# Attention of the first batch in two sweeps over the head pairs, with two loads a pair

## The chip, the cores and the metric

The kernel runs on one core of a Trainium2 chip. Its time is the device time of one execution, in microseconds (us). The engines are TensorE (PE in the rows, its weight loads PEld), VectorE (DVE), ScalarE (ACT), GpSimd (POOL) and SyncE (SP), on whose queue all loads and stores are issued.

## The reference

Three layers follow each other, for B=4 batches of S=576 tokens with H=8 heads of D=64:

```python
a = softmax(causal(q @ k.T / sqrt(D)))
mem = (phi(q) @ M_prev) / (phi(q) @ z_prev + 1e-6)       # phi(x) = elu(x) + 1
x = (sigmoid(beta) * mem + (1 - sigmoid(beta)) * (a @ v)) as [2304, 512]
P = exp(x @ w_gate - max); 8 rounds of row and column normalization
x = sum over e of P[:, e] * (relu(x @ w1[e]) @ w2[e])    # 8 experts, inner width 1024
out = leaky(x @ w_in) @ w_out                            # inner width 2048
```

## The kernel before

**Attention.** `Attention.run` goes over 16 units, a unit being one batch `b` and one pair of heads `hp` (four pairs a batch, called pairs here). A unit has four stages by query tiles of 128 tokens: `(0, 1)`, `(2,)`, `(3,)`, and `(4,)`, the last 64 tokens of both heads at once. In each stage, TensorE computes `scores` (tile `sps`), VectorE masks them and finds the row minimum (line 229), ScalarE takes the exponent with its row sum (line 231). One unit later the same stage of the previous unit is transposed (`turn`, tile `atps`) and copied to `at`, and its features and row factors (`nq`, `spread`) are transposed (`turned`, tile `tps`). When all is there, `outputs` multiplies with `M_prev` and `v` (tile `avps`); VectorE or ScalarE takes `x` out of PSUM, and `xh` (ScalarE, line 280) and `xl` (GpSimd, line 285) are its high and low parts, the operands of all that follows. In batch 0 a row's factors are applied late, by a multiplication with the transposed `R`; in the other batches they are applied to `a` ahead of the transposes.

**Expert 0.** `First.run` computes expert 0 for nine blocks of 256 tokens. A block has 8 steps; a step has 12 matmuls into `ph` (line 485), a relu split into `hh` and `hl`, and 6 matmuls into `po` (line 493). A step is handed out in four parts, so a block has 32. Its weights pass through `Weights`: a 512 KB load to `raw`, ScalarE makes the high part (line 451), GpSimd the low part (line 452), two of each for a load and four for an instance (a quarter of expert 0). `Weights.advance` issues the next of them.

**The order.** A scheduler fixes the order of each engine's queue when the program is built; an instruction waits for its operands and for a free buffer. PSUM tiles of the attention come from a pool with 4 buffers (`pa0`) until batch 0 is done, and with 2 (`pa1`) afterwards, when `First` has its own PSUM. Between the attention's steps `fill` hands out parts of `First`, as many as `FILL` says for the step just taken, as long as their tokens are ready:

```python
for what in steps:
    if isinstance(what, tuple):
        ready = {1: 3, 2: 5, 3: 8}[what[1]]
    else:
        fill(FILL[what], ready)
```

So no part of `First` runs before all four pairs of batch 0 are done. What is left of `First` then runs beside the gate and the normalization rounds, and after them come the other experts and the last layer (`rest`, lines 798 to 868), which take most of the time.

Of the kernel before, what the change touches and what calls it, by code (L numbers as in the profile page):

```python
# [20 lines left out]
P = 128  # L21
# [3 lines left out]
NTT = NT // P  # L25

# [34 lines left out]
class Attention:  # L61
# [6 lines left out]
    def __init__(self, tc, ctx, xh, xl, xd, qt, kt, qn, vn, M_prev, zn, ident, beta):  # L68
        self.tc, self.nc = tc, tc.nc
        self.xh, self.xl, self.xd = xh, xl, xd  # L70
        self.qt, self.kt, self.qn, self.vn, self.M, self.z = qt, kt, qn, vn, M_prev, zn
# [4 lines left out]
        self.pairs = [{"b": b, "hp": hp, "a": {}} for b in range(B) for hp in range(HP)]  # L76
        self.bd = [self.sb.tile([P, P], F32, name=f"bd{i}") for i in range(2)]
        for t in self.bd:
            nc.gpsimd.memset(t, 0.0)
        self.load_qk(self.pairs[0])  # L80
# [8 lines left out]
        for j in range(2):  # L89
            nc.sync.dma_start(out=tail[j * D:(j + 1) * D, 512:], in_=mask[:D, 512:512 + D])  # L90
        self.tail = tail
        self.load_n(self.pairs[0])
        make_identity(nc, ident)
        self.at = self.sb.tile([P, 2, self.WIDE], F32, name="at")
        self.ms = [[self.sb.tile([P, D], F32, name=f"ms{j}{i}") for j in range(2)] for i in range(2)]
        for ms in self.ms:
            for j, t in enumerate(ms):
                nc.gpsimd.memset(t[D - j * D:P - j * D], 0.0)
        self.load_v(self.pairs[0])
# [13 lines left out]

    def big(self, nm):
        return self.ps.tile([P, 1024], F32, tag="big", name=nm)
# [14 lines left out]
    def load_n(self, r):  # L130
        b, hp = r["b"], r["hp"]
        r["p"] = self.sbt([P, 9, D], "nq", bufs=2)
        self.nc.sync.dma_start(out=r["p"], in_=self.qn[b, hp])
        r["z"] = self.sbt([P, 9, D], "nz")
        for j in range(2):
            self.nc.sync.dma_start(out=r["z"][j * D:(j + 1) * D], in_=self.z[b, hp, j:j + 1].to_broadcast([D, 9, D]))

    def load_v(self, r):
        b, hp = r["b"], r["hp"]
        r["v"] = self.sbt([P, 2, 5, D], "nv", bufs=2)  # L140
        self.nc.sync.dma_start(out=r["v"], in_=self.vn[b, hp])
        r["ms"] = self.ms[hp % 2]
        for j in range(2):
            s = slice(j * D, (j + 1) * D)
            self.nc.sync.dma_start(out=r["ms"][j][s], in_=self.M[b, 2 * hp + j])

    def features(self, r):

        nc = self.nc
        ph, z = r["p"], r["z"]  # L150
        ex = self.sbt([P, 9, D], "ex")
        nc.scalar.activation(ex, ph, AF.Exp)
        nc.scalar.activation(ph, ph, AF.Relu)
        exf, phf, zf = (t.rearrange("p c d -> p (c d)") for t in (ex, ph, z))
# [3 lines left out]
        nrm = r["nrm"] = self.sbt([P, 9], "nrm", bufs=2)  # L158
        nc.vector.reduce_sum(nrm, ex, axis=AX.X)
        nc.vector.scalar_tensor_tensor(out=nrm, in0=nrm, scalar=1e-6, in1=self.ginv[:, r["hp"]], op0=ALU.add, op1=ALU.mult)  # L160
# [3 lines left out]
    @staticmethod  # L164
    def late(r):
        return r["b"] == 0

    def rows(self, r):

        nc, sm, nrm, ph = self.nc, r["sm"], r["nrm"], r["p"]  # L170
        late = self.late(r)
        nc.vector.scalar_tensor_tensor(out=sm, in0=sm, scalar=1e-9, in1=self.inv[:, r["hp"]], op0=ALU.add, op1=ALU.mult)
# [3 lines left out]
        halves = [slice(j * D, (j + 1) * D) for j in range(2)]  # L176
        nc.gpsimd.tensor_mul(ph[:, :8], ph[:, :8], nrm[:, :8].unsqueeze(2).to_broadcast([P, 8, D]))
        for s in halves:
            nc.gpsimd.tensor_mul(self.pb[s, s], ph[s, 8], nrm[s, 8:9].to_broadcast([D, D]))
        if late:  # L180
            r["row"] = self.sbt([P, 8, D], "spread")
            nc.gpsimd.tensor_copy(r["row"], sm[:, :8].unsqueeze(2).to_broadcast([P, 8, D]))
            for s in halves:
                nc.gpsimd.tensor_copy(self.rb[s, s], sm[s, 8:9].to_broadcast([D, D]))
            return
# [7 lines left out]
    def turned(self, r):  # L193

        nc = self.nc
        for src, block, nm in ((r["p"], self.pb, "pT"), (r.get("row"), self.rb, "R"))[:1 + self.late(r)]:
            ps = self.big("tps")
            for c in range(4):
                nc.tensor.transpose(ps[:, c * P:(c + 1) * P], src[:, 2 * c:2 * c + 2].rearrange("p h d -> p (h d)"), self.ident)
            nc.tensor.matmul(ps[:, 512:S], block, self.fold, start=True, stop=True)  # L200
            r[nm] = self.sbt([P, S], nm)
            nc.scalar.activation(r[nm], ps[:, :S], AF.Copy)
            yield

    def scores(self, r, ts):

        nc = self.nc
        ps = r["sps"] = self.big("sps")
        q, k = r["q"], r["k"]
        if ts == (4,):  # L210
# [940 lines left out]
```

## Time and profile before

| | |
|---|---|
| time, median of 3 runs (lowest, highest) | 2153.28 us (2150.87, 2156.08) |
| profiled execution: its own time, its span | 2151.47 us, 2149.7 us |
| TensorE busy in the span | 2102.0 us, 98% |
| VectorE, ScalarE, GpSimd busy | 1387.3, 758.2, 1082.9 us |
| first matmul of expert 0 | 77.40 us from the span's start |

Idle time of TensorE is what the span holds beyond its work: with 98% busy there are 47.7 us of it in all. An engine's idle time counts only where TensorE waits for that engine. The profiled execution's own time is its span plus 1.8 us around it, and is 1.8 us below the median.

### The profile page before, as it was taken

How to read it: one execution, taken by the hardware profiler on the slowest of the kernel's cores; microseconds unless marked ns; L12 is line 12 of the kernel's file. 1: busy time of each engine (PE TensorE's matmuls, PEld its weight loads, DVE VectorE, ACT ScalarE, POOL GpSimd, SP SyncE). 2: the span in 40 equal slices, each digit the busy share in tenths (PEclk: the TensorE clock that was granted, in tenths of full speed). 3: DMA queues.
4: the chain of work that ended last, by engine and by line, in shares of the span. 5: the costliest groups of instructions: out<-in, count | busy, mean ns of one | idle time of the engine just before them, and what ended most of it. 6: DMA issues, size and time to landing. Idle time of an engine off the chain costs nothing.

```text
span 2149.7 us, 35269 instructions
## 1 busy us (share of the span) xinstructions
PE 2102.0 (98%) x13841; PEld 1858.8 (86%) x13841; DVE 1387.3 (65%) x2523; ACT 758.2 (35%) x1557; POOL 1082.9 (50%) x1007
## 2 busy tenths in 40 slices
PE   6999999999999999999999999999999999999999
PEld 4677777898899999999999889999999998898998
DVE  6666655358776777677776989745455553566565
ACT  6666652333322222222222243332332323333331
POOL 5322223448744554455544688755555444574650
PEclk9999999999999999999999999999999999999999
DMA  7443412245522221222226444311111152336111
GB/s 220 132 122 118 129 56 72 88 148 167 147 69 69 69 69 55 69 70 69 74 65 249 137 132 153 108 50 50 59 40 60 60 216 72 105 90 243 55 54 40
DMA packets 164582, 217.84 MB, mean 101 GB/s; under 512 B 14144, under 2 KB 109376, under 8 KB 162880
## 3 DMA queue, kind: packets, MB, share of 16 engines
q1 hardware_dynamic: 164416, 215.59, 31.5%
q8 instruction: 109, 1.79, 0.3%
q14 instruction: 57, 0.47, 0.1%
HBM read 166.23 MB, written 49.28 MB: 100 GB/s over the span
## 4 chain that ended last, share of the span: by engine, by line
PE 74%; DVE 4%; POOL 2%; issue 2%; ACT 1%; DMA 0%; DVEq 0%; POOLq 0%; ACTq 0%
PE po L854 38%; PE pq L810 29%; PE pq L798 4%; PE po L493 1%; PE ph L485 1%; DVE hl L829 0%; POOL stl L658 0%; POOL ql L600 0%; DVE c L831 0%; DVE acc L864 0%; DMA raw<-in_moe_w_dram 0%; DVE c L820 0%; POOL w0l L600 0%; PE xt L916 0%; POOL raw L614 0%
## 5 line engine op out<-in xcount | busy, mean ns | idle before, releaser
L854 PE MATMUL po<-w,hh 128*128 128x512 f32 x2592 | 802.4, 391 | 9.3 <-DVE acc L864 4.3
L854 PEld LDWEIGHTS po<-w,hh 128*128 128x128 f32 x2592 | 473.8, 188 | 100.8 <-DVE acc L864 3.8
L854 PE MATMUL po<-w,hl 128*128 128x512 f32 (+1 forms) x1476 | 507.0, 364 | 0.0
L600 POOL TENSOR_TENSOR w0l<-raw,w0h 128x512 fp32r<-128x512 f32 x144 | 191.6, 1351 | 355.6 <-ACT w0h L599 355.1
L854 PEld LDWEIGHTS po<-w,hl 128*128 128x128 f32 x1476 | 277.2, 188 | 58.5
L828 ACT ACTIVATE hh<-c 128x512 fp32r<-128x512 f32 x224 | 129.2, 624 | 478.2 <-DVE c L823 478.2
L810 PE MATMUL pq<-Xh,w0h 128*128 128x256 f32 x960 | 266.7, 278 | 2.1 <-DVE uv L818 1.4
L810 PE MATMUL pq<-Xl,w0h 128*128 128x256 f32 x960 | 265.8, 277 | 0.0
L810 PE MATMUL pq<-Xh,w0l 128*128 128x256 f32 x960 | 265.4, 276 | 0.0
L829 DVE SCALAR_TENSOR_TENSOR hl<-c,hh 128x512 fp32r<-128x512 f32 x224 | 170.1, 800 | 79.1 <-ACT hh L828 79.1
L864 DVE SCALAR_TENSOR_TENSOR acc<-po,Pm,acc 128x512 f32<-128x512 f32 x252 | 176.3, 748 | 47.6 <-PE po L854 45.3
L600 POOL TENSOR_TENSOR w<-raw,w 128x512 fp32r<-128x512 f32 x144 | 198.5, 1396 | 1.0
L818 DVE TENSOR_TENSOR uv<-pq,s 128x256 f32<-128x256 f32 x144 | 60.4, 420 | 189.3 <-ACT s L817 189.1
L810 PEld LDWEIGHTS pq<-Xh,w0h 128*128 128x128 f32 x960 | 180.1, 188 | 2.8 <-DVE uv L818 1.6
L810 PEld LDWEIGHTS pq<-Xl,w0h 128*128 128x128 f32 x960 | 180.6, 188 | 0.0
L810 PEld LDWEIGHTS pq<-Xh,w0l 128*128 128x128 f32 x960 | 180.4, 188 | 0.0
L817 ACT ACTIVATE s<-pq 128x256 f32<-128x256 f32 x144 | 54.8, 381 | 248.1 <-PE pq L810 248.0
L600 POOL TENSOR_TENSOR ql<-raw,qh 128x512 fp32r<-128x512 f32 x48 | 62.6, 1325 | 130.4 <-ACT qh L599 130.4
L810 PE MATMUL pq<-Xh,w1h 128*128 128x256 f32 x384 | 106.1, 276 | 1.1 <-ACT xa L929 1.1
L832 ACT ACTIVATE hh<-c 128x512 fp32r<-128x512 f32 x64 | 40.5, 632 | 186.6 <-DVE c L831 186.6
L810 PE MATMUL pq<-Xh,sh 128*128 128x256 f32 x384 | 106.2, 277 | 0.0
L810 PE MATMUL pq<-Xl,sh 128*128 128x256 f32 x384 | 106.1, 276 | 0.0
(257 smaller groups left out, 4891.0 us busy)
## 6 DMA issues: line engine op xcount, KB each, us to landing
raw<-in_moe_w_dram SPq DMA_DIRECT2D x136, 512.0 KB, 3.5
Xh<-kh SPq DMA_DIRECT2D x6, 1792.0 KB, 7.4
Xl<-kl SPq DMA_DIRECT2D x6, 1792.0 KB, 11.4
f<-in_moe_w_in_dram SPq DMA_DIRECT2D x16, 512.0 KB, 5.0
f<-in_moe_w_out_dram SPq DMA_DIRECT2D x16, 512.0 KB, 4.7
raw<-wide_in SPq DMA_DIRECT2D x16, 512.0 KB, 3.4
raw<-wide_out SPq DMA_DIRECT2D x16, 512.0 KB, 3.7
kh<-sth SPq DMA_DIRECT2D x12, 512.0 KB, 5.2
```

The costliest lines, as they stand in the source:

```text
L485: nc.tensor.matmul(ph[:, :T], wp[:, c, f0:f0 + P], x[:, c, t0:t0 + T], start=(n == 0), stop=(n == 11))
L493: nc.tensor.matmul(po, a[:, s], wp[:, c, :], start=(first and n == 0), stop=(last and n == 2))
L600: self.nc.gpsimd.tensor_sub(lo, src, f32(hi))
L798: nc.tensor.matmul(ph[:, f * SB:(f + 1) * SB], wp(a, c % 2), xp[x][:, c], start=(n == 0), stop=(n == 11))
L810: nc.tensor.matmul(b[-1][:, o:o + SB], wp(a, c), X[s][part][:, x, c], start=(n == 0), stop=(n == 5))
L817: nc.scalar.activation(s1, b[0][:, lo], AF.Copy)
L818: v.tensor_add(uv[:, 0], b[0][:, up], s1)
L828: nc.scalar.activation(hh[:, f], c, AF.Relu)
L829: v.scalar_tensor_tensor(out=hl[:, f], in0=c, scalar=0.0, in1=f32(hh[:, f]), op0=ALU.max, op1=ALU.subtract)
L832: nc.scalar.activation(hh[:, f], c, AF.Copy)
L854: nc.tensor.matmul(po[j][:, d], a[:, f, r], w[1, part][:, f, d], start=(fp == 0 and f == 0 and n == 0), stop=(fp == 1 and f == 1 and n == ...
L864: nc.vector.scalar_tensor_tensor(out=acc[t], in0=po[j], scalar=Pm[:, t0 + t, e:e + 1], in1=acc[t], op0=ALU.mult, op1=ALU.add)
```

## The change

Batch 0 is no longer taken pair by pair. A first sweep takes stage `(0, 1)` alone of the four pairs, to `outputs` and `xl` (a unit "top": tokens 0 to 255), and a second sweep takes stages `(2,)`, `(3,)` and `(4,)` ("rest": tokens 256 to 575). The other batches stay whole ("all"). Behind the first sweep `First` begins, with block 0 alone (`READY["top"]` and the limit of 30 parts), so the second sweep runs with the 2 buffers of `pa1`. `FILL` becomes a table by phase: 7 parts a pair in the second sweep, 8 in batch 1 (12 before), 12 afterwards as before. `W.finish(0)` asks for one instance of weights ahead of `First` where `W.finish(2)` asked for three.

The host now lays out q, k and the block-diagonal q of the last tokens in one array `qk`, and features, `z`, `M_prev` and `v` in another, `pk`, so a unit has two loads with three buffers each; before it had ten (`q`, `k`, two `bd`, `nq`, two `nz`, `nv`, two `ms`) with one or two buffers. Tiles for `bd` and `ms` and their memsets fall away; two small copies that built `tail` become operations of GpSimd. `turned` now writes both transposes into one PSUM tile `tps` and empties it with one copy.

```diff
 class Attention:
...
+        self.pairs = [dict(self.CUTS[cut], b=b, hp=hp, a={}) for b in range(B) for cut in (("top", "rest") if b == 0 else ("all",)) for hp in range(HP)]
+        for r in self.pairs[:2]:
+            self.load_qk(r)
+            self.load_pk(r)
...
+    CUTS = {
+        "all": dict(stages=((0, 1), (2,), (3,), (4,)), g=slice(0, 9), t0=0, n=S, late=False),
+        "top": dict(stages=((0, 1),), g=slice(0, 4), t0=0, n=256, late=True),
+        "rest": dict(stages=((2,), (3,), (4,)), g=slice(4, 9), t0=256, n=320, late=True),
+    }
...
     def load_qk(self, r):
-        b, hp, nc = r["b"], r["hp"], self.nc
-        for nm, src in (("q", self.qt), ("k", self.kt)):
-            r[nm] = self.sbt([P, S], nm, bufs=2)
-            nc.sync.dma_start(out=r[nm], in_=src[b, hp])
-        r["bd"] = self.bd[hp % 2]
-        for j in range(2):
-            s = slice(j * D, (j + 1) * D)
-            nc.sync.dma_start(out=r["bd"][s, s], in_=self.qt[b, hp, s, 512:])
...
+        t = r["qk"] = self.sbt([P, QK], "qk", bufs=3)
+        cut = slice(0, 512) if r["n"] == 256 else slice(r["t0"], QK)
+        self.nc.sync.dma_start(out=t[:, cut], in_=self.qk[r["b"], r["hp"], :, cut])
+
+    def load_pk(self, r):
+        pk = self.sbt([P, 30, D], "pk", bufs=3)
+        cut = slice(0, 14) if r["n"] == 256 else slice(8 if r["t0"] else 0, 30)
+        self.nc.sync.dma_start(out=pk[:, cut], in_=self.pk[r["b"], r["hp"], :, cut])
...
     def turned(self, r):
 
-        nc = self.nc
-        for src, block, nm in ((r["p"], self.pb, "pT"), (r.get("row"), self.rb, "R"))[:1 + self.late(r)]:
-            ps = self.big("tps")
-            for c in range(4):
-                nc.tensor.transpose(ps[:, c * P:(c + 1) * P], src[:, 2 * c:2 * c + 2].rearrange("p h d -> p (h d)"), self.ident)
-            nc.tensor.matmul(ps[:, 512:S], block, self.fold, start=True, stop=True)
-            r[nm] = self.sbt([P, S], nm)
-            nc.scalar.activation(r[nm], ps[:, :S], AF.Copy)
+        nc, n, m = self.nc, r["n"], 1 + r["late"]
+        ps = self.big("tps")
+        step = 256 if n == 256 else 512
+        for k, (src, block) in enumerate(((r["p"], self.pb), (r.get("row"), self.rb))[:m]):
+            for c in range(n // P):
+                o = k * step + c * P
+                nc.tensor.transpose(ps[:, o:o + P], src[:, 2 * c:2 * c + 2].rearrange("p h d -> p (h d)"), self.ident)
+            if n != 256:
+                o = k * step + n - D
+                nc.tensor.matmul(ps[:, o:o + D], block, self.fold, start=True, stop=True)
             yield
+        both = self.sbt([P, 2 * 320], "pT")
...
+        nc.scalar.activation(out, src, AF.Copy)
...
     def run(self):
...
+                if k == 0 and len(old) == 1:
+                    for _ in turned:
+                        pass
+                    self.outputs(prev)
+                    if prev["hp"] == HP - 1:
+                        yield ("top", 0)
+                yield 2 if ts != (4,) else 4
...
-FILL = {1: 1, 2: 1, 4: 2, 5: 1, 7: 2}
...
+FILL = {"top": {2: 1, 4: 2, 5: 1}, 0: {1: 1, 2: 1, 5: 1}, 1: {1: 1, 2: 1, 4: 2, 5: 1}, 2: {1: 1, 2: 1, 4: 2, 5: 1, 7: 2}}
+READY = {"top": 0, 0: 1, 1: 3, 2: 5, 3: 8}
...
                 with tc.tile_pool(name="pa0", bufs=4, space=PSUM) as att.ps:
-                    W = None
-                    for what in steps:
-                        if W is None:
+                    for n, what in enumerate(steps):
+                        if n == 4:
                             W = Weights(tc, wp, w1, w2, seq)
-                        elif what == 4:
-                            W.advance(2)
-                        if what == ("done", 0):
+                        elif n > 8 and W.ahead == 0:
+                            W.advance(1)
+                        if what == ("top", 0):
                             break
-                    W.finish(2)
+                    W.finish(0)
...
                 def fill(n, limit):
                     for _ in range(n):
-                        if at_block[0] > limit:
+                        if limit < 8 and parts[0] >= 32 * limit + 30:
                             return
```

TensorE at the start of expert 0, before: the last rows are `outputs` of the fourth pair with all its tokens, then `ph` of the first step.

```order
L268 MATMUL avps<-pT,ms_116 64x320
L268 MATMUL avps<-pT,ms_117 64x320
L271 MATMUL avps<-at,nv 64x320 x6
L271 MATMUL avps<-at,nv 64x192 x2
L271 MATMUL avps<-at,nv 64x64 x2
L485 MATMUL ph<-xh,w0h_155 128x256
L485 MATMUL ph<-xl,w0h_155 128x256
L485 MATMUL ph<-xh,w0l_156 128x256
L485 MATMUL ph<-xh,w0h_155 128x256
```

The same place now: `outputs` of the fourth pair with 256 tokens, then the first step of `First`, with scores of the second sweep (`sps`) between.

```order
L275 MATMUL avps<-pT,pk 64x256 x2
L278 MATMUL avps<-at,pk 64x256 x2
L278 MATMUL avps<-at,pk 64x128 x2
L504 MATMUL ph<-xh,w0h_172 128x256
L504 MATMUL ph<-xl,w0h_172 128x256
L504 MATMUL ph<-xh,w0l_173 128x256
L504 MATMUL ph<-xh,w0h_172 128x256
L504 MATMUL ph<-xl,w0h_172 128x256
L504 MATMUL ph<-xh,w0l_173 128x256
L216 MATMUL sps<-qk 128x512 x2
L504 MATMUL ph<-xh,w0h_172 128x256
L504 MATMUL ph<-xl,w0h_172 128x256
```

Behind `outputs` of 256 tokens instead of 576, `ph` follows at once, and the second sweep stands inside expert 0.

TensorE in the second sweep, its first to second pair: transposes of the features (`tps<-ident,pk`), then of the row factors (`tps<-ident,spread`).

```order
L190 MATMUL tps<-ident,pk 128x128 x2
L193 MATMUL tps<-fold,pb 128x64
L504 MATMUL ph<-xh,w0h_176 128x256
L504 MATMUL ph<-xl,w0h_176 128x256
L504 MATMUL ph<-xh,w0l_177 128x256
L504 MATMUL ph<-xh,w0h_176 128x256
L504 MATMUL ph<-xl,w0h_176 128x256
L504 MATMUL ph<-xh,w0l_177 128x256
L190 MATMUL tps<-ident,spread 128x128 x2
L255 MATMUL atps<-ident,a_453 128x128 x4
L255 MATMUL atps<-ident,a_456 128x128 x4
L193 MATMUL tps<-fold,rb 128x64
```

The tile `tps` is opened at its first row and is complete only behind the transposes of stage 3 (`atps`, eight of them), where `fold,rb` closes it; before, each `tps` was opened and closed at one place.

GpSimd before, from its first low part of weights on.

```order
L452 TENSOR_TENSOR w0l_156<-raw_167,w0h_155 128x512 x2
L452 TENSOR_TENSOR w_0_157<-raw_169,w_0_157 128x512
L177 TENSOR_TENSOR nq<-nq,nrm 128x512
L179 TENSOR_TENSOR pb<-nq,nrm 64x64 x2
L182 COPY spread<-sm 128x512
L184 COPY rb<-sm 64x64 x2
L452 TENSOR_TENSOR w_0_157<-raw_169,w_0_157 128x512
L452 TENSOR_TENSOR w0l_160<-raw_225,w0h_159 128x512 x2
L452 TENSOR_TENSOR w_1_161<-raw_256,w_1_161 128x512
L177 TENSOR_TENSOR nq<-nq,nrm 128x512
L179 TENSOR_TENSOR pb<-nq,nrm 64x64 x2
```

GpSimd now, behind the first `xl` of the first sweep (`w0l` and `w_1` are low parts of weights, `pk<-pk,nrm` scales the features, `spread` the row factors).

```order
L166 TENSOR_TENSOR pk<-pk,nrm 128x256
L171 COPY spread<-sm 128x256
L471 TENSOR_TENSOR w0l_177<-raw_318,w0h_176 128x512 x2
L296 TENSOR_TENSOR xl<-x,xh 128x256
L471 TENSOR_TENSOR w_1_178<-raw_328,w_1_178 128x512
L166 TENSOR_TENSOR pk<-pk,nrm 128x256
L171 COPY spread<-sm 128x256
L471 TENSOR_TENSOR w_1_178<-raw_328,w_1_178 128x512
L296 TENSOR_TENSOR xl<-x,xh 128x256
L471 TENSOR_TENSOR w0l_181<-raw_476,w0h_180 128x512 x2
L471 TENSOR_TENSOR w1l_183<-raw_509,w1h_182 128x512 x2
L296 TENSOR_TENSOR xl<-x,xh 128x256
```

The low parts of the weights now stand between the `xl` of the first sweep; before, they stood between the pairs ahead of expert 0.

SyncE's queue at the program's start, before and now.

```order
L124 DMA q<-in_qt_dram 128x576
L124 DMA k<-in_kt_dram 128x576
L128 DMA bd_85<-in_qt_dram 64x64 x2
L133 DMA nq<-in_qn_dram 128x576
L136 DMA nz<-in_zn_dram 64x576 x2
L141 DMA nv<-in_vn_dram 128x640
L145 DMA ms_114<-in_M_prev_dram 64x64
L145 DMA ms_115<-in_M_prev_dram 64x64
L106 DMA g<-in_beta_dram 128x36
L1015 DMA wgr<-in_moe_w_gate_dram 128x4x8
L124 DMA q<-in_qt_dram 128x576
```

```order
L124 DMA qk<-in_qk_dram 128x512
L129 DMA pk<-in_pk_dram 128x896
L124 DMA qk<-in_qk_dram 128x512
L129 DMA pk<-in_pk_dram 128x896
L101 DMA g<-in_beta_dram 128x36
L1035 DMA wgr<-in_moe_w_gate_dram 128x4x8
L124 DMA qk<-in_qk_dram 128x512
L129 DMA pk<-in_pk_dram 128x896
L455 DMA raw_184<-in_moe_w_dram 128x4x256
L455 DMA raw_186<-in_moe_w_dram 128x2x512
```

Two loads a unit stand where ten stood, and the table `g` is issued behind the loads of two units instead of one.

## Rows read from the trace of the kernel before

**Rows 1.** The page: the chain that ended last, shares of the span by engine.
```profile
PE 74%; DVE 4%; POOL 2%; issue 2%; ACT 1%; DMA 0%; DVEq 0%; POOLq 0%; ACTq 0%
```

**Rows 2.** Stretches: busy us (instructions) PE, PEld, DVE, ACT, POOL; granted clock, DMA share, GB/s.
```profile
0.00:77.40 77.40, 57.55 (x393) 37.30 (x393) 53.83 (x159) 55.77 (x139) 37.61 (x62) 0.93 0.69 198
77.40:81.16 3.76, 3.76 (x19) 3.76 (x20) 0.25 (x1) 1.04 (x2) 1.42 (x1) 0.55 0.37 141
81.16:305.00 223.84, 220.41 (x1537) 166.72 (x1537) 139.90 (x409) 142.38 (x345) 53.78 (x60) 1.00 0.36 109
```

**Rows 3.** Timeline of TensorE: start, duration, line, tile, count, idle time before.
```profile
46.92 0.88 PE L249 MATMUL atps<-ident,a 128*128 128x128 f32 x6
47.73 0.93 PE L218 MATMUL sps<-k,q 64*128 64x128 f32 x8
48.59 0.66 PE L199 MATMUL tps<-ident,nq 128*128 128x128 f32 x4
49.08 0.33 PE L200 MATMUL tps<-fold,pb 128*128 128x64 f32 x2
...
58.76 0.65 PE L268 MATMUL avps<-pT,ms 128*64 128x256 f32 x4
...
59.90 0.71 PE L268 MATMUL avps<-pT,ms 128*64 128x320 f32 x4
...
62.59 0.88 PE L249 MATMUL atps<-ident,a 128*128 128x128 f32 x6
...
65.67 0.92 PE L218 MATMUL sps<-k,q 64*128 64x384 f32 x4
...
68.24 1.13 PE L218 MATMUL sps<-k,q 64*128 64x512 f32 x4
...
72.64 2.23 PE L271 MATMUL avps<-at,nv 128*64 128x320 f32 x20
77.40 0.50 PE L485 MATMUL ph<-xh,w0h 128*128 128x256 f32 x1 [2.54 <-DVE x L279]
```

**Rows 4.** Stretch after TensorE's first pause, and six transposes inside it.
```profile
20.00:25.00 5.00, 3.58 (x16) 2.82 (x16) 0.00 (x0) 2.59 (x8) 4.72 (x9) 0.50 0.95 287
...
22.65 1.49 PE L249 MATMUL atps<-ident,a 128*128 128x128 f32 x6
```

**Rows 5.** TensorE's waits: in total, times, longest; 0 to 110 us, then 77.4 to 305.
```profile
PE tps L199 <- POOL nq L177: 7.5, 1, 7.5
...
PE sps L212 <- DVE nm__921 L229: 0.8, 1, 0.8
```

**Rows 6.** GpSimd's groups by shape, 0 to 80 us: count, busy us, mean ns.
```profile
L452 POOL TENSOR_TENSOR w<-raw,w 128x512 fp32r<-128x512 f32 x4 | 5.1, 1271 | 5.3 <-ACT w L451 5.2
...
L177 POOL TENSOR_TENSOR nq<-nq,nrm 128x512 f32<-128x512 f32 x6 | 6.3, 1056 | 16.4 <-DVE nrm L174 9.8 <-DVE nrm L161 6.6
...
L285 POOL TENSOR_TENSOR xl<-x,xh 128x576 fp32r<-128x576 f32 x4 | 5.6, 1412 | 4.8 <-ACT xh L280 4.8
...
L182 POOL COPY spread<-sm 128x512 f32<-128x512 f32 x4 | 2.4, 611 | 0.3
```

**Rows 7.** DMA, 0 to 80 us: KB each, median us to landing.
```profile
raw<-in_moe_w_dram SPq DMA_DIRECT2D x8, 512.0 KB, 3.7
```

**Rows 8.** Timeline of ScalarE and GpSimd: first features, first low part of weights.
```profile
6.38 0.68 ACT L152 ACTIVATE ex<-nq 128x576 f32<-128x576 f32 x1 [4.37 <-DMA nq<-in_qn_dram]
...
16.60 2.55 POOL L452 TENSOR_TENSOR w0l<-raw,w0h 128x512 fp32r<-128x512 f32 x2 [11.87 <-ACT w0h L451]
```

**Rows 9.** VectorE, one multiply at two times, and GpSimd beside the first.
```profile
38.17 1.33 DVE L156 TENSOR_TENSOR ex<-nq,nz 128x576 f32<-128x576 f32 x1
...
49.97 0.76 DVE L156 TENSOR_TENSOR ex<-nq,nz 128x576 f32<-128x576 f32 x1 [1.24 <-DMA nz<-in_zn_dram]
...
38.83 3.02 POOL L452 TENSOR_TENSOR w0l<-raw,w0h 128x512 fp32r<-128x512 f32 x2
```

More of the change, by code (lines that the diff above doesn't have):

```diff
@@ L89, in __init__ @@
         for j in range(2):
-            nc.sync.dma_start(out=tail[j * D:(j + 1) * D, 512:], in_=mask[:D, 512:512 + D])
+            t = tail[j * D:(j + 1) * D, 512:]
+            nc.gpsimd.affine_select(out=t, in_=t, pattern=[[-1, D]], compare_op=ALU.is_ge, fill=-8.0e9, base=0, channel_multiplier=1)
         self.tail = tail
-        self.load_n(self.pairs[0])
         make_identity(nc, ident)
         self.at = self.sb.tile([P, 2, self.WIDE], F32, name="at")
[L95 to L99, printed above, removed]
         self.pb, self.rb = (self.sb.tile([P, P], F32, name=n) for n in ("pb", "rb"))
@@ L273, in outputs @@
-        group(256, 0, 256, ((0, 1600, 256), (1, 1472, 128)))
-        group(512, 256, 320, ((0, 64, 320), (1, 384, 320), (2, 704, 320), (3, 1152, 192), (4, 0, 64)))
-        x = self.sbt([P, S], "x")
-        hp, c0 = r["hp"], r["b"] * S
-        xh = self.xh[:, hp, c0:c0 + S]
-        if self.late(r):
-            nc.vector.tensor_mul(x, av[:, 256:256 + S], r["R"])
+                    nc.tensor.matmul(av[j * D:(j + 1) * D, o + nq - sn:o + nq], r["v"](j, c), at[:, j, s0:s0 + sn], start=False, stop=i == len(parts) - 1)
@@ new lines, in outputs @@
+        o, n = self.first_tiles(r), r["n"]
+        if r["t0"] == 0:
+            group(256, 0, 256, ((0, o + P, 256), (1, o, 128)))
+        if n != 256:
+            group(512, 256, 320, ((0, 64, 320), (1, 384, 320), (2, 704, 320), (3, 1152, 192), (4, 0, 64)))
+        x = self.sbt([P, S], "x")[:, :n]
+        hp, c0 = r["hp"], r["b"] * S + r["t0"]
+        src = av[:, 256 + r["t0"]:256 + r["t0"] + n]
+        xh = self.xh[:, hp, c0:c0 + n]
+        if r["late"]:
+            nc.vector.tensor_mul(x, src, r["R"])
@@ L301, in run @@
+            for k, ts in enumerate(r["stages"]):
+                turn = (lambda: self.turn(prev, old[k])) if k < len(old) else lambda: None
+                lo = None if top else turn()
                 yield 1
@@ L319, in run @@
             yield 5
-            if nxt is not None:
-                self.load_v(nxt)
+            if n + 2 < len(pairs):
+                self.load_pk(pairs[n + 2])
             yield 4
@@ L324, in run @@
         turned = self.turned(prev)
-        for ts in self.STAGES:
+        for ts in prev["stages"]:
             lo = self.turn(prev, ts)
@@ L1050, in body @@
                         if isinstance(what, tuple):
-                            ready = {1: 3, 2: 5, 3: 8}[what[1]]
+                            seen = what[1]
                         else:
-                            fill(FILL[what], ready)
+                            fill(FILL[seen].get(what, 0), READY[seen])
             rp = right.enter_context(tc.tile_pool(name="rp", bufs=1, side="right"))
```

153 lines of the change are left out of this document (80 added, 73 removed).

## The prediction

> **What bounds the kernel now.** The page's chain shows TensorE with 74% of the span [rows 1], and over the whole span it is busy 98%; so only what TensorE loses can be won back, and the change touches only the start. The busy times by stretch say where the loss lies: up to 77.40 us TensorE is busy 57.55 us of 77.40 [rows 2], while ScalarE (55.77) and VectorE (53.83) are as busy as it is. The timeline gives the price of the work itself: the fourth pair of batch 0 runs from 62.59 to the end of the row at 72.64, that is 12.28 us, without a wait of TensorE [rows 3]. Four such pairs are 49.1 us. So the opening loses 77.4 - 49.1 = 28.3 us, by idle time and by work at the low clock. The waits show the largest single piece, 7.5 us in which the first pair's features are awaited from GpSimd [rows 5]. Two more losses follow. The first matmul of expert 0 comes 2.54 us after TensorE fell idle [rows 3], and up to 81.16 us the granted clock is 0.55 [rows 2], nearly all of it at the lower of the two levels (1.2 GHz): 0.45 x 3.76 = 1.7 us. From there to 305 us, which is nearly all of batches 1 to 3, TensorE is idle 223.84 - 220.41 = 3.4 us [rows 2]. In all, 28.3 + 1.7 + 3.4 = 33.4 us are lost by 305 us.
>
> **The change, part by part.** TensorE's work stays: the same products and transposes are made in other places. What counts is the same loss, worked out anew.
>
> The first sweep. A pair's share of it is the transposes of stage `(0, 1)` (46.92 to 47.73, 0.81 us), the scores (to 48.59, 0.86), the feature transposes (to 49.08, 0.49) and the outputs of 256 tokens (58.76 to 59.90, 1.14) [rows 3]: 3.3 us, 13.2 for four pairs. The four pairs cannot fill TensorE, so the sweep's end is set by the other engines, and by GpSimd most of all: the twelve low parts of three weight instances, which before lay ahead of expert 0 within 77 us, stand between the `xl` of the sweep, and the last `xl` stands behind all of them, as the change's order shows. A low part takes 1.27 us, an `xl` of 576 tokens 1.41, so one of 256 about 0.63; scaling 512 columns of features 1.06 and spreading the factors 0.61, half of both here, 0.83 together [rows 6]. From the first low part on that is 12 x 1.27 + 4 x 0.63 + 2 x 0.83 = 19.4 us.
>
> When does it begin? The first low part ran at 16.60 us before, and the first features at 6.38, when 0.9 MB had landed [rows 8]. Now a load of `qk` (262 KB) and one of `pk` (459 KB) a pair, for three pairs, and 1.05 MB of weights lie ahead of that low part: 3.2 MB. At the 198 GB/s of the opening [rows 2] and with 1 us to the first byte that is 17.3 us. Then there are waits: a `raw` tile is free again after its second low part, the next load takes 3.7 us to land [rows 7] and a conversion about 0.6, against some 4 us of other work on GpSimd in between; and the last `xl` needs `xh` from ScalarE, which is behind two conversions. I take 3.3 us for these. So the last `xl` of the sweep is ready at 17.3 + 19.4 + 3.3 = 40.0 us. Without any wait it would be 36.7; with larger loads moving no faster and every `raw` late by 2 us, 45. The nine products of the first three pairs can run before it, so expert 0 starts about 2 us earlier but is held at the fourth pair's.
>
> By 40.0 us TensorE has done 13.2 us of the sweep, the scores of stages `(2,)` and `(3,)` of the second sweep's first pair (0.92 and 1.13, [rows 3]) and ten products of expert 0 (19 instructions in 3.76 us at clock 0.55 [rows 2] make 0.11 each at the full clock, 1.1). That is 16.3 us; 23.7 are lost.
>
> The clock. After 7.5 us of idling TensorE ran at 0.50, six transposes took 1.49 us [rows 4] where they take 0.88 [rows 3], and after 2.54 us of idling it ran low again. With 13.2 us of work in some 36, the sweep's own work may run low without harm, since GpSimd sets the end. What costs is the lower level when expert 0 begins: between nothing and the 1.7 us of before; I take the middle, 0.8. The Trainium skill ("TensorE: Matmul & The Clock Gate", Part 1) says that the engine's clock is halved after it has been idle and is given back only by sustained work, which the trace bears out in both pauses; by that rule the price would be the full 1.7, and the sum 2150.8 instead of the 2149.9 below.
>
> The second sweep. Stages `(2,)` to `(4,)` cost 12.28 - 3.3 = 9.0 us of TensorE a pair, and 7 parts of expert 0 stand beside them. ScalarE and VectorE have less to do per pair than in 62.59 to 72.64, where TensorE never waited for them [rows 3]. But the attention has two PSUM buffers here instead of four, and `tps` holds one of them from stage `(2,)` past the transposes of stage `(3,)`. Under two buffers the trace shows single waits of 0.8 us at most, on VectorE's drain of scores [rows 5]. I take one such wait for each of the first two pairs and a third of it for each of the others, 2.1 us. The lower bound is nothing (no row of 62.59 to 72.64 has a wait), the upper is in the rivals.
>
> Batches 1 to 3 keep 3.4 us. Batch 1 has 8 parts a pair beside it instead of 12, which gives less cover, but the waits after 81 us that stood at expert 0's first steps have moved into the second sweep; I let them cancel. The gate, the normalization and the start of the other experts follow the same work in the same order, so they keep their waits.
>
> Costed at nothing: two loads instead of ten a pair (SyncE is awaited only for what has to land, and the bytes are nearly the same), the memsets that go and the two small operations that come on GpSimd (it is idle ahead of 16.60 us, [rows 8]), and the one copy for both transposes on ScalarE in place of two. If ScalarE were the bound of the second sweep, that copy would count, as a small gain.
>
> The sum: 23.7 + 0.8 + 2.1 + 3.4 = 30.0 us lost instead of 33.4, a gain of 3.4. Against the profiled execution's own 2151.47 us that is 2148.1; the median of the runs stands 1.8 above that execution, so 2149.9 against 2153.28. A change of 0.2% (4.3 us) is about what a measurement of this kernel can tell from none, so the forecast is just inside it.
>
> **The rivals.**
>
> A faster opening. If the larger, more regular loads run faster than 198 GB/s, the first low part starts at 16 us and no `raw` is late: the last `xl` at 37 us, and with no wait in the second sweep the gain is 3.4 + 3.0 + 2.1 = 8.5, 2144.8 us. For it: a 512 KB load lands in 3.7 us [rows 7], which is more than 198 GB/s even with its latency. Against it: VectorE and ScalarE also have a chain to run through for each pair, from features to row factors, before anything can be scaled.
>
> GpSimd and VectorE slow each other. Beside two low parts a multiply of VectorE took 1.33 us instead of 0.76, and the two low parts took 3.02 instead of 2.54 [rows 6, 9], 0.24 each. In the sweep GpSimd is busy without a pause while VectorE makes the features of pair after pair. Twelve low parts longer by 0.24 put the last `xl` 2.9 us later, at 42.9: gain 0.5, 2152.8 us. The Trainium skill ("GPSIMD Engine Reference", section 1, Specifications) says that GpSimd's SBUF interfaces are shared with VectorE and that operations with two SBUF inputs contend; the three rows agree.
>
> The slower side: PSUM in the second sweep. Per stage TensorE needs a buffer for scores and one for transposes, and with `tps` open one is left; each further stage then waits for a copy of VectorE or ScalarE that itself queues behind the features of the next pair, which wait for `pk`. It decides from (4.3 + 3.4 + 2.1) / 4, about 2.4 us a pair; at 3.5 us a pair, three copies of about 1 us and their hand-over, the second sweep loses 14 us and the time is 2149.9 + 14 - 2.1 = 2161.8. For it: nothing in the trace ran with this hold; against it: expert 0's parts stand between the stages, and under two buffers all of 81.16 to 305 us holds only 3.4 us of idle time [rows 2].
>
> **How the numbers follow.** The forecast has a chance of 0.46, from 2146 to 2153 by its own bounds, of which 0.20 lie more than 0.2% below the median of before and 0.26 within. The faster opening has 0.22. The shared interface has 0.12 (0.09 within, 0.03 beyond on the slow side), the PSUM hold 0.20 (0.17 slower, 0.03 within). So faster 0.42, same 0.38, slower 0.20. For 8 in 10 the range reaches from 2143, past the faster opening, to 2158, which takes in the sweep ending at 45 us and a mild PSUM hold.
>
> **What the profile will show.** If the steps are right: the first product of expert 0 at 37 to 39 us and no idle time of TensorE from about 40 us on beyond 0.8 us at a time; GpSimd without a pause from 17 us to the last `xl`; the granted clock low over most of 10 to 38 us; the second sweep and block 0 of expert 0 done near 97 us (behind 40.0 us, 33.9 us of attention, some 20 of expert 0 and the 2.9 of the two losses). The forecast is wrong if TensorE waits in the second sweep for copies of `at` or `pT` at every stage (slower), or if expert 0 runs unbroken from 36 us (faster). A difference behind 320 us would be outside all of these steps.

## The result and the profile after

The changed kernel takes 2170.05 us (median of 4 runs, 2167.78 to 2172.14) beside 2154.68 for the kernel before in the same comparison: ratio 1.0072, 95% interval 1.005 to 1.0093. It is slower by 15.4 us; 2149.9 was forecast, and the range ended at 2158. The profiled execution has a span of 2167.2 us, 17.5 more than before's 2149.7.

The page's chain of the changed kernel, which answers to [rows 1]: VectorE, ScalarE, GpSimd and DMA have each taken a larger share of it.

```profile
PE 76%; DVE 8%; POOL 4%; ACT 4%; issue 3%; DMA 3%; SPq 0%; DVEq 0%; POOLq 0%; ACTq 0%
```

Busy times of the changed kernel by stretch, with the columns of [rows 2]: up to expert 0's first product, its first products, the second sweep, batches 1 to 3.

```profile
0.00:36.92 36.92, 19.64 (x124) 12.43 (x124) 24.46 (x88) 23.43 (x67) 22.92 (x37) 1.00 0.71 236
36.92:41.20 4.28, 4.28 (x16) 2.64 (x17) 2.14 (x5) 1.44 (x4) 3.19 (x3) 0.60 0.99 377
41.20:104.80 63.60, 60.80 (x404) 43.53 (x402) 37.07 (x108) 37.60 (x91) 18.66 (x35) 1.00 0.39 130
104.80:344.50 239.70, 228.24 (x1587) 167.65 (x1588) 148.19 (x415) 144.55 (x350) 53.75 (x60) 1.00 0.32 103
```

In the second sweep TensorE is idle for 2.8 us. In batches 1 to 3 it is idle for 11.5 us, where the kernel before lost 3.4 in almost the same part of the program [rows 2] (and still 3.4 with the stretch taken to its attention's end at 320.7 us). That is the surprise of the result: the stretch that the prediction let cancel holds most of the loss.

Busy time counts a matmul at the low clock as work, so a second count is used below. **Time lost by t** is t less the work that TensorE has done by then, with each matmul taken at the distance that its line and shape usually has to the next one (the median in the kernel before from 82 us on). Changes from one kind of product to another count as lost too, some 1.4 us a pair even where nothing waits. In us, worked out from all matmul rows of the five profiles (the three kernels on the right are experiments below). Each column is one execution: those of loads_placed and hold took 2.5 and 2.3 us less than the median of their kernel, that of placed_phase 2.5 more, so the last rows carry differences of that size.

| by | before | changed | loads_placed | hold | placed_phase |
|---|---|---|---|---|---|
| 37 us | 20.5 | 24.8 | 20.2 | 24.3 | 25.0 |
| 81 us | 32.1 | 32.4 | 28.9 | 33.7 | 34.2 |
| 100 us | 35.2 | 34.5 | 30.7 | 36.8 | 36.3 |
| 180 us | 41.6 | 45.8 | 36.8 | 44.9 | 46.7 |
| end of the attention | 53.9 | 68.0 | 46.6 | 55.2 | 59.3 |
| first product of the later experts | 68.2 | 84.1 | 62.2 | 69.5 | 73.8 |
| end | 94.8 | 112.5 | 90.4 | 97.2 | 103.0 |

Read the two columns on the left. At 100 us the changed kernel is ahead by 0.7 us; at the attention's end it is behind by 14.1, and the normalization and the later experts add 3.6.

**What holds TensorE in batches 1 to 3.** Its waits there, as in [rows 5] (in total, times, longest), and below them the longest of ScalarE:

```profile
PE sps L216 <- ACT pT L198: 4.9, 5, 1.4
PE sps L209 <- DVE nm__1888 L231: 1.7, 1, 1.7
PE sps L209 <- DVE nm__2525 L231: 1.4, 1, 1.4
...
ACT ex L144 <- DMA pk<-in_pk_dram: 17.9, 6, 4.0
```

One such place in the timeline of the changed kernel (start, duration, engine, line, idle time before): SyncE's request, ScalarE, TensorE.

```profile
199.40 0.33 SPq L129 DMA_DIRECT2D pk<-in_pk_dram  x1
...
201.00 0.38 ACT L516 ACTIVATE hh<-ph 128x256 fp32r<-128x256 f32 x1 [0.88 <-PE ph L504]
205.35 0.68 ACT L144 ACTIVATE ex<-pk 128x576 f32<-128x576 f32 x1 [3.97 <-DMA pk<-in_pk_dram]
205.94 0.39 ACT L233 ACTIVATE a<-a,nm__2109 128x128 f32<-128x128 f32 x1
...
207.70 0.63 ACT L198 ACTIVATE pT<-tps 128x576 f32<-128x576 f32 x1
...
208.38 0.92 PE L216 MATMUL sps<-qk 64*128 64x384 f32 x4 [1.39 <-ACT pT L198]
```

ScalarE stands still for 3.97 us at `ex`, the first instruction of the features of a coming pair, because its load was requested at 199.40 us and has not landed. The exponentials of this pair and the copy `pT` are queued behind it. `pT` empties one of the two PSUM buffers, and the next scores need it. The kernel before has the other order at the same step of a pair:

```profile
207.29 0.33 SPq L133 DMA_DIRECT2D nq<-in_qn_dram  x1
...
208.83 0.63 ACT L202 ACTIVATE pT<-tps 128x576 f32<-128x576 f32 x1
209.36 0.79 ACT L260 ACTIVATE at<-atps 128x768 f32<-128x768 f32 x1
210.97 0.69 ACT L152 ACTIVATE ex<-nq 128x576 f32<-128x576 f32 x1 [0.82 <-DMA nq<-in_qn_dram]
```

There `ex` waits too, but only 0.82 us, and `pT` is done by then. The DMA rows (KB, median us to landing) of the changed kernel's batches, and under them of the kernel before, show that the larger load takes longer to land:

```profile
pk<-in_pk_dram SPq DMA_DIRECT2D x10, 960.0 KB, 5.5
...
nq<-in_qn_dram SPq DMA_DIRECT2D x9, 288.0 KB, 2.8
```

But the load is not late against the kernel before. `pk` is requested at 199.40 us, beside the row that takes the previous pair's `x` out (199.46), and `ex` has it 5.9 us behind that row; `nq` is requested 5.0 us behind the same row of its pair (202.26), and `ex` has it after 8.7. The load is late only for an `ex` that stands further forward.

### The profile page after: what moved, and what is told of

Read it like the earlier page. It is cut to its first block, busy times and chain, and to the rows that moved or that the text cites. A ratio compares the mean times of both kernels' runs of the same rounds, so it can differ in the third digit from the quotient of the medians.

```text
span 2167.2 us, 35177 instructions
## 1 busy us (share of the span) xinstructions
PE 2109.8 (97%) x13841; PEld 1855.7 (86%) x13841; DVE 1401.0 (65%) x2559; ACT 758.9 (35%) x1569; POOL 1085.5 (50%) x1015
## 4 chain that ended last, share of the span: by engine, by line
PE 76%; DVE 8%; POOL 4%; ACT 4%; issue 3%; DMA 3%; SPq 0%; DVEq 0%; POOLq 0%; ACTq 0%
PE po L873 36%; PE pq L829 27%; PE pq L817 4%; PE po L512 2%; PE ph L504 2%; PE avps L278 2%; ACT a L233 1%; DMA pk<-in_pk_dram 1%; DVE a L231 1%; PE sps L216 1%; PE avps L275 1%; DMA raw<-in_moe_w_dram 1%; DVE hl L848 1%; PE atps L255 1%; DMA xa<-xd 1%
## 5 line engine op out<-in xcount | busy, mean ns | idle before, releaser
L847 ACT ACTIVATE hh<-c 128x512 fp32r<-128x512 f32 x224 | 129.2, 624 | 479.6 <-DVE c L842 479.6
L829 PE MATMUL pq<-Xh,sl 128*128 128x256 f32 x384 | 106.0, 276 | 0.0
## 6 DMA issues: line engine op xcount, KB each, us to landing
Xl<-kl SPq DMA_DIRECT2D x6, 1792.0 KB, 11.5
```

Source lines behind the costliest of these rows:

```text
L829: nc.tensor.matmul(b[-1][:, o:o + SB], wp(a, c), X[s][part][:, x, c], start=(n == 0), stop=(n == 5))
L847: nc.scalar.activation(hh[:, f], c, AF.Relu)
```

## The experiments

Theory T1: the large load is late for `ex`, and what is queued behind `ex` on ScalarE is late for TensorE; after the first runs it is narrowed to T1b, that the order made by the scheduler does it and not the load in itself. The rivals: T2, the number of parts of expert 0 in a pair and their phase against the pairs; T3, the copy `pT` written one step later; T5, the large loads cost by themselves; T6, thin cover in batch 1. All medians are of 4 to 11 runs. The kernel before was measured anew in each of four comparisons, with medians from 2152.94 to 2155.17 us, so runs are compared below by what each lies over the kernel before of its own comparison; on that scale the changed kernel is at +15.4.

| run | us | over the kernel before, us | ratio, 95% interval |
|---|---|---|---|
| split | 2172.23 | +18.6 | 1.0085 (1.0071 to 1.0099) |
| early | 2169.57 | +15.9 | 1.0068 (1.0056 to 1.0081) |
| fill | 2171.30 | +17.6 | 1.0084 (1.007 to 1.0098) |
| loads | 2160.98 | +7.3 | 1.0034 (1.0021 to 1.0048) |
| placed | 2162.04 | +9.1 | 1.0051 (1.0039 to 1.0064) |
| loads_placed | 2149.56 | -3.4 | 0.9983 (0.9974 to 0.9992) |
| phase | 2161.36 | +8.4 | 1.0039 (1.0026 to 1.0051) |
| placed_phase | 2157.08 | +4.1 | 1.002 (1.0011 to 1.0029) |
| placed_all | 2160.85 | +6.6 | 1.0032 (1.002 to 1.0044) |
| thin | 2149.80 | -4.5 | 0.9982 (0.9973 to 0.9991) |
| hold | 2155.93 | +0.8 | 1.0004 (0.9995 to 1.0013) |
| shift | 2155.20 | 0.0 | 1.0000 (0.9991 to 1.0008) |

**The loads alone (loads).** The kernel before, with the ten loads of a pair replaced:

```diff
+        t = r["qk"] = self.sbt([P, QK], "qk", bufs=3)
+        self.nc.sync.dma_start(out=t, in_=self.qk[r["b"], r["hp"]])
...
+        pk = self.sbt([P, 30, D], "pk", bufs=3)
+        self.nc.sync.dma_start(out=pk, in_=self.pk[r["b"], r["hp"]])
```

> The kernel before (one sweep over batch 0, its table of parts, its code for the transposes of the features) with the two loads a pair alone: q, k and the block-diagonal q tail in one tile, features, z, M and v in another, three buffers each, requested where the changed kernel does so. T1: in ScalarE's order ex stands ahead of the exponentials here too in the second half of the attention part, so the loads alone cost what the changed kernel lost in batches 1 to 3: 2160 to 2166 us, with ScalarE waiting for the load at ex, and the scores for pT. T2 and T3 (nothing of the loads is at fault): no slower than the kernel before, 2150 to 2156.

Measured: 2160.98 us, 7.3 over the kernel before, in one sweep. TensorE's and ScalarE's waits of this run from 100 to 327.5 us show the same pair of rows as the changed kernel:

```profile
PE sps L196 <- ACT pT L179: 8.1, 9, 1.7
...
ACT ex L129 <- DMA pk<-in_pk_dram: 13.3, 9, 2.2
```

So the loads, costed at nothing, do this without the two sweeps.

**An earlier load (split).** Features and z in a tile and a load of their own:

```diff
+        pn = self.sbt([P, 18, D], "pn", bufs=3)
+        self.nc.sync.dma_start(out=pn[:, :2 * n], in_=self.pk[r["b"], r["hp"], :, o:o + 2 * n])
...
                 self.load_qk(pairs[n + 2])
+                self.load_pn(pairs[n + 2])
```

> The changed kernel with the second load of a pair cut in two tiles: the columns of the features (p and z, 18 of 30) in a load of their own, which is requested beside the load of q and k and has its buffer back as soon as the pair's transposes are done; M and v (12 of 30) stay in the load at the pair's end. In the order of the program that the scheduler makes, ex then stands behind the four exponentials and the copy pT of the first stage and no longer ahead of them. Theory T1 (the 960 KB load is asked for only when the pair before last has given its v back, ScalarE waits 2.4 to 4.0 us for it at the head of its queue, and the copy pT behind it keeps a PSUM buffer from the scores): the waits of the scores on pT (1.6, 1.1, 1.2, 1.1, 0.8 and 0.5 us by the distances between TensorE's rows, 6.2 in all) go, so 2163 to 2165 us, and down to 2158 if the waits of the fourth stage on VectorE follow from the same delay. T2 (the number of parts laid into a pair and First's position decide) and T3 (the copy pT comes one step later in the code): no change, 2168 to 2172.

A miss: 2172.23 us. The waits for `pT` are gone, but others are there. The timeline of this run (SyncE, ScalarE, VectorE, TensorE):

```profile
229.72 0.33 SPq L143 DMA_DIRECT2D pn<-in_pk_dram  x1
...
234.40 0.69 ACT L151 ACTIVATE ex<-pn 128x576 f32<-128x576 f32 x1 [1.59 <-DMA pn<-in_pk_dram]
...
235.89 0.76 DVE L154 SCALAR_TENSOR_TENSOR pn<-ex,pn 128x576 f32<-128x576 f32 x1 [1.67 <-ACT pn L152]
...
240.57 1.24 PE L216 MATMUL sps<-qk 128*128 128x320 f32 x4 [1.03 <-DVE nm__2351 L238]
```

An earlier load did not get slack. For the last pair it was requested at 274.4 us where the rest of the pair's data followed at 290.5, and the scheduler moved the features forward with it: the last `ex` stands nearly a whole pair ahead of its place in the changed kernel. There the features wait again: ScalarE 1.59 us and VectorE 1.67, and the scores of the last tile wait 1.03 us for VectorE. It is the place of the features in the queues that counts, not the buffers alone.

**The copy one step earlier (early)** and **12 parts a pair (fill):**

```diff
                 nc.tensor.matmul(ps[:, o:o + D], block, self.fold, start=True, stop=True)
-            yield
+            if k < m - 1:
+                yield
```

> The changed kernel with the copy pT of batches 1 to 3 written in the same step as its transposes, as in the kernel before, instead of one step later. T3 (the PSUM buffer of the transposes is held a step longer and so the scores wait): the waits of the scores on pT go, 2163 to 2165 us. T1: ex still stands ahead of the exponentials and of pT in ScalarE's order and waits for its load, so no change, 2168 to 2172.

```diff
-FILL = {"top": {2: 1, 4: 2, 5: 1}, 0: {1: 1, 2: 1, 5: 1}, 1: {1: 1, 2: 1, 4: 2, 5: 1}, 2: {1: 1, 2: 1, 4: 2, 5: 1, 7: 2}}
+FILL = {"top": {2: 1, 4: 2, 5: 1}, 0: {1: 1, 2: 1, 4: 2, 5: 1, 7: 2}, 1: {1: 1, 2: 1, 4: 2, 5: 1, 7: 2}, 2: {1: 1, 2: 1, 4: 2, 5: 1, 7: 2}}
```

> The changed kernel with 12 parts of expert 0 laid into each pair of batch 1 and the pairs after it, as in batches 2 and 3 and in the kernel before, instead of 8 (the limits by tokens that are ready are left). T2: the excess of batch 1 over the kernel before (3 to 4 us of the loss between 105 and 176 us) goes and the phases of the later batches fall as before: 2160 to 2166 us. T1 and T3: within 2 us of the changed kernel, 2168 to 2172, and ScalarE's waits on the load of pk stay, some of them in batch 1 now.

Neither moves the time. The row of TensorE's wait for `pT` in early, then the rows in fill:

```profile
PE sps L217 <- ACT pT L199: 4.8, 5, 1.5
```

```profile
PE sps L216 <- ACT pT L198: 8.7, 7, 1.9
...
ACT ex L144 <- DMA pk<-in_pk_dram: 24.5, 7, 4.5
```

The step of the copy in the code is not at fault (T3 falls). More parts a pair only bring more waits behind `ex`, so of T2 the number of parts falls and the phase is left.

**The order alone (placed, loads_placed).** One edge of order for ScalarE, nothing else: `ex` is queued behind the copy `at` of the third score tile.

```diff
+        ins = nc.scalar.activation(to(self.at), src, AF.Copy)
+        if ts == (2,):
+            self.copies.append(ins.ins)
...
+        behind = self.copies[-2:-1] if r["b"] else []
+        with self.tc.issue_after(behind[0]) if behind else ExitStack():
+            nc.scalar.activation(ex, ph, AF.Exp)
```

> The changed kernel with nothing but an order: in ScalarE's queue the first activation of the features of the next pair (ex) is put behind the copy at of the present pair's third score tile, where the kernel before had it; the load, its size and its time of request stay. Theory T1b (it is not the load's lateness in itself, but that the scheduler then puts the features' instructions at places where a late operand stops the queue): ex no longer stands ahead of the exponentials, the load has landed by then, the waits of the scores on the copy pT (6.2 us by the distances between rows) go: 2162 to 2166 us. T2 (the number of parts in a pair and First's phase against the pairs): no change, 2168 to 2172.

> The kernel before with the two loads a pair, as in the run loads (2161.0 us), and the same order for ex. T1b: the 8.1 us that the scores waited for the copy pT go, 2151 to 2155 us, which is the kernel before or a little under it, since the opening keeps the 2.6 us that the fewer loads give. A rival, T5 (the large loads themselves cost, by what they take from the transfers beside them or by their landing): no lower than 2158.

Both moved as T1b said: placed is 6.3 us better than the changed kernel (its five runs spread from 2161.03 to 2168.78), loads_placed 10.7 better than loads and 1.4 below its range, and in neither does TensorE wait for `pT` any more in batches 1 to 3. T5 falls: the same large loads with that order are 3.4 us faster than the kernel before. thin, below, is as fast within the noise, and no kernel of the study is faster than these two. ScalarE's timeline of loads_placed has `pT` first and `ex` without a wait:

```profile
223.73 0.62 ACT L182 ACTIVATE pT<-tps 128x576 f32<-128x576 f32 x1
224.26 0.79 ACT L241 ACTIVATE at<-atps 128x768 f32<-128x768 f32 x1
224.95 0.67 ACT L132 ACTIVATE ex<-pk 128x576 f32<-128x576 f32 x1
```

Busy time in about the last 11 pairs of loads and of loads_placed: idle 9.8 us in the first, 0.4 in the second.

```profile
98.50:327.50 229.00, 219.16 (x1520) 166.36 (x1519) 132.62 (x377) 132.08 (x320) 50.69 (x56) 0.99 0.31 100
```

```profile
92.00:313.40 221.40, 220.98 (x1566) 169.20 (x1566) 134.07 (x387) 136.16 (x327) 52.60 (x57) 1.00 0.34 109
```

**The phase of expert 0 (phase, shift, placed_phase).** A step of expert 0 has four parts. Before, each pair of batches 2 and 3 began at a whole step; after the second sweep's 31 parts and batch 1's eights it begins two parts later. VectorE's remainder `hl` then stands between other instructions, and the features' sum ahead of the maxima of the fourth score tile.

```diff
                             seen = what[1]
+                            if seen == 1:
+                                fill(2, READY[seen])
```

> The changed kernel with expert 0 set forward by two of its parts at the end of batch 1, so that in batches 2 and 3 each pair begins at the same of the four parts of a step of expert 0 as in the kernel before (VectorE's relu remainder of expert 0 then stands where it stood before). T2: the waits of the fourth stage's scores on VectorE (5.6 us by the distances) go, 2164 to 2167 us, while the waits for pT stay. T1b alone: within 2 us of the changed kernel, 2168 to 2172.

> The changed kernel with both, and the sum of the features on VectorE put behind the maxima of the present pair's fourth score tile: on ScalarE and VectorE the instructions of a pair of batches 2 and 3 then stand in the order of the kernel before. If order is all of it, batches 2 and 3 lose what they lost before (13.5 us instead of 23.3 by the distances between TensorE's rows): 2158 to 2163 us, and what is left over the kernel before lies ahead of 200 us, in the normalization and in the experts behind. If large loads or the two sweeps cost something else in these batches, 2165 or more.

> The run loads_placed (2149.6 us, one sweep) with expert 0 set forward by two parts at the end of batch 1, the reverse of the run phase: in batches 2 and 3 a pair then begins in the middle of a step of expert 0, as in the changed kernel, and VectorE has the features' sum and the relu remainder at the changed kernel's places. T2: the pairs of batches 2 and 3 lose 0.3 to 0.5 us more each, as in the run placed against placed_phase (9.3 and 5.6 us in the two batches instead of 7.7 and 4.9): 2151 to 2155 us. If the phase costs nothing by itself: 2148 to 2151.

All three moved the way that T2 expected: phase is 7.0 us better than the changed kernel (2.6 below its range), shift 3.4 worse than loads_placed (5.6 by the medians alone), and order and phase together, with one more edge for the features' sum on VectorE, leave 4.1 over the kernel before. TensorE's waits in phase: those for `pT` are still there but shorter, the long ones on VectorE are gone.

```profile
PE sps L216 <- ACT pT L198: 3.2, 5, 1.3
...
PE sps L209 <- DVE nm__2535 L231: 0.4, 1, 0.4
```

Not all of it lies in the pairs: of shift's loss the lost time puts 2.6 us into batches 2 and 3 and 3.2 into the normalization. The busy times of batches 1 to 3 in placed, phase and placed_phase stand against the 239.70 and 228.24 us above: idle 3.6, 6.3 and 2.5 us instead of 11.5.

```profile
104.50:335.80 231.30, 227.75 (x1587) 167.68 (x1588) 146.45 (x415) 144.54 (x350) 54.02 (x60) 1.00 0.33 107
```

```profile
104.80:340.50 235.70, 229.43 (x1597) 171.99 (x1598) 144.25 (x415) 144.90 (x350) 54.92 (x60) 1.00 0.32 105
```

```profile
106.40:337.20 230.80, 228.26 (x1597) 172.15 (x1598) 143.71 (x416) 144.81 (x350) 53.97 (x60) 1.00 0.33 107
```

By the count of lost time, placed_phase loses 12.6 us in batches 2 and 3, the changed kernel 23.3, the kernel before 13.5. In this part of the program order and phase are all of it.

**What the two sweeps are worth (placed_all, thin, hold).** placed_all orders the features in the second sweep too, where one wait of 1.2 us had the same cause, and moves expert 0 to a whole step at the end of batch 0 as well (`fill(1 + seen, READY[seen])` for `seen < 2`). thin is loads_placed with the changed kernel's 8 parts while only batch 0 is ready. hold is the two sweeps with the order edges of placed_all, expert 0 kept back until batch 0 is whole, and 12 parts a pair from there. The first two lines are of hold, the last two of thin:

```diff
+FULL = {1: 1, 2: 1, 4: 2, 5: 1, 7: 2}
+FILL = {"top": {}, 0: FULL, 1: FULL, 2: FULL}
...
+THIN = {1: 1, 2: 1, 5: 1}
+                            fill((THIN if ready == 1 else FILL).get(what, 0), ready)
```

> The run placed_phase (2157.1 us) with the same order for the features in the second sweep as well (there the load of pk held ex back by 2.1 us and the scores waited 1.2 us for the copy behind it), and expert 0 set forward by one part at the end of batch 0 too, so that the pairs of batch 1 begin at a whole step of expert 0. T1b and T2: 1 to 3 us less, 2154 to 2157 us, still over the kernel before, since the thin cover of batch 1 stays. If the two sweeps' rest is only order and phase, 2153 or less.

> The run loads_placed (2149.6 us, one sweep) with 8 parts of expert 0 in each pair of batch 1 and the first of batch 2 instead of 12, which is what the changed kernel has there because its second sweep has already taken 31 of the 62 parts that the tokens of batch 0 allow. T6 (thin cover: with fewer products beside it, a pair's chain from scores to products lies bare at its joints): the pairs of batch 1 lose 1.7 to 2.7 us each instead of 1.4 to 1.8, so 2152 to 2155 us. If the cover doesn't matter there, 2148 to 2151.

> The two sweeps and the two loads, the features' instructions kept in order in both sweeps, but expert 0 held back until batch 0 is whole, and from there the kernel before's table of 12 parts a pair. Against loads_placed (2149.6 us) this is what the second pass over the pairs costs by itself, against placed_phase (2157.1 us) what the early expert 0 gives back. If the early start is worth what the prediction took (TensorE filled from 37 us on), this run is slower than placed_phase by 5 us or more, 2162 to 2172. If the gain was never there, since single pairs lose little after 37 us anyway, it lies within 3 us of placed_phase, 2154 to 2160.

placed_all is a miss: 2160.85 us, with runs from 2155.62 to 2164.44. The wait in the second sweep stayed (its `pT` row is still 1.2 us, and `ex` still waits for `pk` there, up to 2.0 us), so the edge did not do there what it was meant to, and nothing was won. thin is a miss for T6: 2149.80, no change, though in its profile the pairs concerned lose 1.8 to 2.1 us each instead of 1.4 to 1.8. hold lies 0.8 us over the kernel before, beside placed_phase at 4.1 and placed_all, which has the same edges, at 6.6: starting expert 0 at 37 us instead of behind batch 0 gains nothing, and may cost. hold and placed_phase stand 4.1 and 7.5 us over loads_placed, which has the same loads and order in one sweep. The table of lost time says where: hold is behind loads_placed by 4.1 us at 37 us, 6.1 at 100 and 8.1 at 180.

## Why the prediction was wrong

**The opening: right in its steps, wrong in what it was set against.** Expert 0's first product was forecast for 37 to 39 us, the last `xl` at 40.0, bound by GpSimd from 17.3 us. GpSimd's first low part and last `xl`, and two rows of TensorE:

```profile
16.70 2.86 POOL L471 TENSOR_TENSOR w0l<-raw,w0h 128x512 fp32r<-128x512 f32 x2
...
39.13 0.98 POOL L296 TENSOR_TENSOR xl<-x,xh 128x256 fp32r<-128x256 f32 x1
```

```profile
36.92 0.38 PE L504 MATMUL ph<-xh,w0h 128*128 128x256 f32 x1 [1.90 <-DVE x L290]
37.15 0.28 PE L504 MATMUL ph<-xl,w0h 128*128 128x256 f32 x1
...
37.83 2.08 PE L216 MATMUL sps<-qk 64*128 64x512 f32 x4
```

36.92 us, and 39.13 + 0.98 = 40.1: both times held. Yet GpSimd did not hold TensorE there. The first product waited for VectorE, which empties the fourth pair's `x` out of PSUM, and TensorE was busy without a break from 36.92 to 41.20 us, so the last `xl` kept it from nothing. The rival of a faster opening had one premise right: the loads moved at 236 GB/s up to 36.92 us instead of 198, and the first low part came at 16.70. But its argument from a 512 KB load was miscounted (3.7 us is 142 GB/s, not more than 198), and GpSimd, busy 20.65 of the 23.41 us up to its last `xl`, still waited for high parts of the weights (1.12 and 0.91 us). The rival of the shared interface took 2.9 us; two of the six pairs of low parts ran longer (2.86 and 2.99 us instead of 2.50), 0.85 us in all.

What failed is the worth of that start. Its gain was taken from the 28.3 us that the opening lost up to 77.40, as if an early expert 0 would spare most of what comes after 40 us. The table shows otherwise: the kernel before had lost 20.5 us by 37 us and only 11.6 more by 81. The changed kernel lost 4.3 more at the front and 7.6 from 37 to 81. At 100 us 0.7 us of gain is left instead of the 3.4 forecast, and hold, without the early start, is no slower than placed_phase with it.

**The clock: 0.8 was too little.** From 36.92 to 41.20 us the granted clock is 0.60 at full occupation, 0.40 x 4.28 = 1.7 us. The Trainium skill ("TensorE: Matmul & The Clock Gate", Part 1), by which the full 1.7 was due, agrees with this row; half of it had been taken.

**The second sweep: held.** 2.1 us of idle time forecast, 2.8 measured. The rival of the PSUM buffers named the right mechanism, a copy queued behind features that wait for `pk`, in the wrong place: one wait of 1.2 us in the second sweep, far below its 3.5 a pair, and five in batches 2 and 3.

**"Batches 1 to 3 keep 3.4 us ... I let them cancel": the step that failed.** They kept 11.5 by idle time. By the table 21.1 us lie between the gain forecast (3.4) and the loss of the profiled execution (17.7): 2.7 up to 100 us, 14.8 from there to the attention's end, 3.6 behind it. Two causes of the middle part were shown by putting each right alone: the place of `ex` (placed, 6.3 us) and expert 0's phase against the pairs (phase, 7.0). Together they give back 11.2 of the 15.4 us (placed_phase). Some of it is one and the same loss, since phase shortens the waits for `pT` too; how much, these runs do not tell.

**"Costed at nothing: two loads instead of ten": failed too.** SyncE was looked at, and what waits for a landing was not followed to ScalarE's queue. The loads alone cost 7.3 us, through the order that the scheduler made of them; with the old order the same loads gain 3.4. The Trainium skill ("DMA: Bandwidth & Descriptors", Rules for kernel authors) advises to merge small transfers into one large one. By these runs that pays here (3.4 us), but only when the first reader is kept behind other work: the merged load lands in 5.5 us, the piece that is read first had taken 2.8.

**"They keep their waits": partly.** The 3.6 us behind the attention are split about evenly between normalization and later experts. The normalization lost 14.3 to 15.0 us in five profiles (before, phase, placed_phase, placed_all, hold), 15.6 to 16.2 in six and 18.7 to 19.0 in three (fill, placed, shift); phase lies at the low end and shift at the high one, but placed, which has the changed kernel's phase, is at 19.0 where that is at 16.1; that expert 0's phase has a part in it is not shown. The later experts' loss varies between 26.6 and 31.8 us without a pattern that these runs tell apart.

**A sign that was not seen.** The clock column was to show the low level over most of 10 to 38 us; it says 1.00 up to 36.92 (the last section has what the durations say).

**Open.** Why the two passes lose more than one up to 180 us was placed, not taken apart: eight passes have eight chains from scores to products, and each is shorter; that is argued only. Thin cover was tried and does not show in the time.

## What to carry to other kernels

When transfers are merged, ask which instruction reads them first, where the scheduler will put that instruction, and what is queued behind it on its engine; a hidden load is hidden only as long as its first reader stands behind other work. Where a part of the work moves against another, check at what step of the one each round of the other now begins: here a shift by two parts moved the time by 7.0 us in one kernel and 3.4 in another, the merged loads alone by 7.3. And set a gain in an opening against what the old kernel lost up to the same time, not against all that its opening lost.

## What the runs showed of the hardware

The low clock did not come with the first product after the pause but later: in the changed kernel the six products from 36.92 us on have the duration of the full clock (0.28 us from the second on), and from 37.83 the four scores of 512 columns take 2.08 us instead of 1.13 [rows 3]. And the clock column is no guide to the first microseconds: it says 1.00 up to 36.92 us, but six transposes took 1.51 us at 12.72 and 0.88 at 25.21.

```profile
12.72 1.51 PE L255 MATMUL atps<-ident,a 128*128 128x128 f32 x6 [4.10 <-ACT a L233]
...
25.21 0.88 PE L255 MATMUL atps<-ident,a 128*128 128x128 f32 x6
```
